# The opening of a fused spectral-filter and max-out kernel: an earlier sine, a row fix on another engine, split evacuations, and later x loads

## The chip, the cores and the metric

The kernel runs on one core of a Trainium2 chip. The time is device microseconds of one execution. An engine is named as in the profile: PE (matmul; PEld its weight loads), DVE (vector), ACT (scalar activation), POOL (GpSimd), SP (the queue that only issues DMAs).

## The reference: what is computed

```python
X = np.fft.rfft(x, axis=1)                  # x: 8 batches x 3072 x 256
y = np.fft.irfft(X * F, n=3072, axis=1)     # F = filt_r + 1j * filt_i, 1537 x 256
h = np.maximum(y @ w1, y @ w2)              # 24576 tokens, 256 -> 1024
out = h @ w_out                             # 1024 -> 256, float32
```

## The kernel before, in words

The transforms are done as matmuls with tables of sines. A length of 3072 is split as 96 times 32: a 96-point transform over one index (`f1`, in batch 0 `s1t`, from batch 2 on `s1` with folded inputs), an exchange of axes, then per frequency group a small transform with table `U` (`s2`), the product with the filter `F` (`products`), the inverse small transform with tables `VP` and `VQ` (`s3`, in batch 0 `s3t`), another exchange, and the inverse 96-point transform with table `G1` (`s4`, later `s4g`), which leaves y for a tile of 384 tokens, transposed. There are 8 tiles in a batch and 64 in all. The max-out layer uses max(a, b) = max(a - b, 0) + b: `moe_h` multiplies y by `Wd` = w1 - w2 and clips at 0, `moe_o` multiplies that by `Wo` and adds y times `M` = w2 w_out. `M` is made in the kernel from transposes of `w2b` (`prep_t`, lines 300 to 306) and a product (`prep_m`).

The order is written out by hand. An **opening** makes the tables and does the transforms of batch 0 without leaving the chip: `s1t` for 8 chunks of x, the transposes `t1` ("T1"), `table_v` and `put_v`, `s2`, the products, `s3t` for v = 1, 0, 2, 3, 4, 5, whose result is evacuated into the tile `zT`, and the transposes `t2` of zT into `zr`, which `s4` reads. Then a loop (lines 777 to 798) walks the 64 tiles in 8 steps each, a step having one `moe_h` (two matmuls), three or four matmuls of `moe_o` of the tile before, and whatever `todo` and `mid` hold for that step. These two lists are filled by `plan`, `plan_f1` and `plan_f2`: step numbers count from 0 to 63 within a batch. In batch 0 they hold, among others: `f1` of batch 1 (chunks 4 to 15 at steps 5 to 12) and its exchange read `f1_read` at step 13; `prep_t(0)` at step 7, `prep_t(1)` at step 8, `prep_m` at step 9; `load_xf` and `fold` of batch 2, which fetch x as float32 into one of three buffers XF and add and subtract halves on POOL; and `visit`, which does `s2`, the products and `s3` of the next batch from step 25 on.

What sets the order of the work around the change:

- Every engine works through its own instructions in program order and waits on semaphores. A DMA is issued from a queue of the engine that issues it: x chunks as bfloat16 (`load_x`), the filter and `Wo` from POOL, between POOL's computing; the raw filter rows, w1 and w2 (tile `WS`), the exchanges, and XF from SP.
- PSUM has eight banks: six in the pool `ps`, two in `pso`. A tile's first matmul waits until the bank's former content has been evacuated.
- In the filter table F, row 32 of the first frequency is special (the Nyquist row): `fix_f` (line 144) writes it over what `double_f` has copied there (line 128, four copies on DVE).
- The two halves of `U` are made by `sines_u(0)` and `sines_u(1)` on ACT (line 249). `table_v(0, ..)` and `s2` of v = 0 to 2 need the first, `table_v(1, ..)` and `s2` of v = 3 to 5 the second.
- `products` (line 657) gives each v two tiles: the first from PSUM on DVE; the second for v = 0, 2, 3, 4 on POOL from a copy `xs` that ACT makes (`stage_x`), for v = 1 on DVE, and for v = 5 shared between DVE (lines 396, 397) and POOL (line 398).
- `spin` and the extra matmuls of line 581 compute nothing that is used; they keep PE occupied.
- On POOL, after the products: `load_x(1, 2, 2)`, `load_wo`, `prep_wd(0)`, two more `load_x`, `prep_wd(1)` to `(3)`, then `cast_w2`, which makes the two halves of `w2b`, then `table_ct`. `prep_wd(q)` makes columns 256q to 256q + 255 of Wd, which `moe_h` needs from step 2q on.

Of the kernel before, what the change touches and what calls it, by code (L numbers as in the profile page):

```python
# [8 lines left out]
FP32 = mybir.dt.float32  # L9
BF16 = mybir.dt.bfloat16  # L10
AF = mybir.ActivationFunctionType
# [4 lines left out]
D = 256  # L16
HID = 1024
NP = 96
NM = 32
NW = 12  # L20
NU = 24
TWO_PI = 6.283184
# [5 lines left out]
def kernel(  # L28
# [23 lines left out]
    F = const.tile([128, 2, NW, 2, D], BF16)  # L52
# [24 lines left out]
    xb = {}  # L77

    def x_tile(b, c):
        if c % 2 == 0:  # L80
            xb[b] = xpool.tile([128, 8, D], BF16, tag="xb", name="xb")
        return xb[b][:, 4 * (c % 2):4 * (c % 2) + 4]

    def load_x(b, c, n):
        for k in range(c, c + n):
            xb[b, k] = x_tile(b, k)[0:NP]
        src = x[b].rearrange("(p m) d -> p m d", m=NM)
        m0 = 4 * (c % 2)
        G.dma_start(out=xb[b][0:NP, m0:m0 + 4 * n], in_=src[:, 4 * c:4 * c + 4 * n, :])  # L89
# [42 lines left out]
    FZ = XF[0][0:33, 0]  # L132
# [9 lines left out]
        G.tensor_copy(F[0:32, ri, 0, 0], FZ[0:32, ri])  # L142

    def fix_f():
        V.tensor_copy(F[32:33, 0, 0, 0], FZ[32:33, 0])


    V.memset(W1, 1.0)
    zero = init.tile([128, 1], FP32)
# [4 lines left out]
    jb = init.tile([128, 16], FP32)  # L154
    cid = init.tile([128, 128], FP32)

    hv = init.tile([128, 2, 1], FP32)
    load_x(0, 0, 1)
    G.iota(pid, pattern=[[1, 1]], base=0, channel_multiplier=1, allow_small_or_imprecise_dtypes=True)
# [32 lines left out]

    def table_ct():
        G.memset(CT, 0.0)
# [52 lines left out]
    def sines_u(h):  # L247
        uv = ua.rearrange("p u c s j -> p u (c s j)")
        S.activation(U[:, NW * h:NW * h + NW], uv[:, NW * h:NW * h + NW], AF.Sin, bias=zero, scale=TWO_PI)

    def table_g():
        pg = ps.tile([96, NP], FP32, tag="ps", name="pg")
        TE.matmul(pg, C1, I128[0:NP, 0:NP], start=True, stop=True)
        S.activation(G1, pg, AF.Copy)

    def table_v(h, q):
# [36 lines left out]
    def load_wo():  # L293
        G.dma_start(out=Wo, in_=moe_w_out.rearrange("(c p) j -> p c j", p=128))

    def prep_wd(q, engine):
        js = slice(256 * q, 256 * q + 256)
        engine.tensor_tensor(Wd[:, :, js], w1f[:, :, js], w2f[:, :, js], OP.subtract)
# [18 lines left out]
    bt = {}  # L317
# [2 lines left out]
    zd = {}  # L320
    at_ = {}

    def f1(b, c, engine):
        if c == 0:
# [3 lines left out]
        at = at_[b]  # L328
        pa = ps.tile([96, 2, D], FP32, tag="ps", name="pa")
        TE.matmul(pa, C1, xb[b, c // 2][:, 2 * (c % 2):2 * (c % 2) + 2], start=True, stop=True)  # L330
# [9 lines left out]
    def f1_read(b):  # L340
        bt[b] = bpool.tile([128, NU, D], BF16, tag="bt", name="bt")
        src = ad[b].rearrange("(u q) m d -> (q m) u d", q=4)
        for u0, u1 in ((0, 4), (4, 12), (12, NU)):
            nc.sync.dma_start(out=bt[b][:, u0:u1], in_=src[:, u0:u1])


    def s1(b, c):
# [140 lines left out]
    po = {}  # L488
# [86 lines left out]
            V.tensor_copy(bt[0][:, 4 * n:4 * n + 4], pb)  # L575

    def s3t(v, pq):
        pool, tag = (ps, "ps") if v % 2 else (pso, "po")
        pz = [pool.tile([128, 2, 2, 2, 2, NM], FP32, tag=tag, name="pt%d" % g) for g in range(2)]
        for _ in range(2 if v == 1 else 1):  # L580
            TE.matmul(pz[0].rearrange("p i s r c m -> p (i s r c m)"), W1[:, 0:128], W1, start=True, stop=True)  # L581
        for i in range(2):
            for s in range(2):
                for dc in range(2):
                    for q, tab in enumerate((VP, VQ)):
                        for g in range(2):
                            TE.matmul(pz[g][:, i, s, :, dc], pq[s][64 * g:64 * g + 64, q, i, 128 * dc:128 * dc + 128],  # L587
                                      tab[64 * g:64 * g + 64, 2 * v + i, s].rearrange("p (r m) -> p r m", r=2),
                                      start=(q == 0), stop=(q == 1))
        zv = zT.rearrange("p c m (w g) q -> p w g (c m) q", g=2)  # L590
        for g in range(2):
            o_ = zv[:, 2 * v:2 * v + 2, g]
            i_ = pz[g].rearrange("p i s r c m -> p i (c m) (s r)")
            if v >= 4 and g == 1:
                V.tensor_copy(o_, i_)
            else:
                S.activation(o_, i_, AF.Copy)

    def t2(c, engines):
        if c == 0:  # L600
            zr[0] = zrpool.tile([96, NM, D], BF16, tag="zr", name="zr")
        n = 4 // len(engines)
        for k, engine in enumerate(engines):
            pr = ps.tile([96, n, D], BF16, tag="ps", name="pr")
            m0 = 4 * c + n * k
            for m in range(n):
                for dc in range(2):
                    TE.transpose(pr[:, m, 128 * dc:128 * dc + 128], zT[:, dc, m0 + m].rearrange("p u q -> p (u q)"),  # L608
                                 I128)
            if engine is V:  # L610
                V.tensor_copy(zr[0][:, m0:m0 + n], pr)
            else:
                S.activation(zr[0][:, m0:m0 + n], pr, AF.Copy)

    def spin(n):
        for _ in range(n):
            pd = ps.tile([128, 512], FP32, tag="ps", name="pd")
            TE.matmul(pd, W1[:, 0:128], W1, start=True, stop=True)  # L618
# [84 lines left out]
    table_ct()  # L703
# [16 lines left out]

    todo = {}
# [1 line left out]
    def plan(b, step, fn, *a):  # L723
        todo.setdefault((b + step // 64, step % 64), []).append((fn, a))

    def plan_f1(b, nb, steps, read):
        for c, n in zip(range(4, 16), steps):
            plan(b, n, f1, nb, c, S if c % 2 == 0 else V)
        plan(b, read, f1_read, nb)

    mid = {}

# [15 lines left out]
            plan(b, steps[-1] + (6 if b else 11), s1_read, b + 2)  # L748

    plan(0, 1, t2, 1, (V,))  # L750
    plan(0, 7, prep_t, 0)
    plan(0, 9, prep_m)
    for c, n in ((2, 7), (4, 22), (5, 32), (6, 40), (7, 48)):
        plan(0, n, t2, c, (V,))
    plan_f1(0, 1, (5, 6, 7, 7, 9, 9, 10, 10, 11, 11, 12, 12), 13)
    plan_f2(0, (25, 28, 31, 35, 38, 42, 46), ((0,), (), (1,), (2,), (3,), (4,), (5, 6)),
            (8, 8, 10, 12, 17, 20, 24, 28), (10, 13, 16, 20, 24, 27, 30, 33))
    for b in range(1, B - 1):
        first = b == 1
        plan_f2(b, (15 if first else 14, 19 if first else 18, 23, 31, 34 if b < B - 2 else 35, 39, 47),  # L760
# [16 lines left out]
    for tt in range(8 * B + 1):  # L777
        b, i = divmod(tt, 8)
        k = 0
        for j in range(8):  # L780
# [48 lines left out]
```

## Time and profile before

| what | us |
|---|---|
| median of 3 runs (lowest, highest) | 497.7 (496.92, 498.1) |
| the profiled execution, its own time | 498.64 |
| its span, from the first instruction to the last | 496.8 |
| first `moe_h` matmul, from the span's start | 37.73 |
| first matmul of `prep_t(0)` | 41.64 |
| first matmul of `moe_o` | 44.19 |
| granted PE clock, mean over the span | 0.989 |

All times within the kernel are counted from the start of the span. The profile's views give, for each instruction or group of equal instructions, the engine, the line, the tiles written and read, the start and the duration; the idle time of the engine ahead of it, and what ended that idle time. `<-` stands between what is written and what is read. A table by stage gives the busy time of each engine and the granted share of PE's clock. A matmul's end is modelled, so that overlapping matmuls can fill a stage to 100%.

The DMAs of w1 and w2 are issued by SP at 25.07, 25.71, 26.25 and 26.76 us; each lands in sixteen parts, the last of them at 29.5, 33.42, 35.3 and 36.6 us. x chunk 2 of batch 1 is issued by POOL at 32.95 and lands at 39.76, Wo at 33.51 and 44.07, x chunks 4 and 6 at 35.65 and 45.71, 36.20 and 48.05.

### The profile page before, as it was taken

The numbers are of one execution on the slowest core, as the hardware profiler recorded it, in microseconds if no ns is written. First come the engines' busy times: TensorE is split into PE (matmuls) and PEld (weight loads), VectorE is DVE, ScalarE is ACT, GpSimd is POOL, SyncE is SP. The second block draws the span as 40 slices with busy tenths as digits, with TensorE's granted clock in tenths as the row PEclk, the third lists the DMA queues.
The fourth block names the chain that finished last, engine by engine and source line by source line (L and its number), as shares of the span: only waits on it lengthen the run. The fifth ranks groups of instructions, "written<-read, shape, count | busy, mean of one in ns | idle before, by whom it ended". The sixth has DMA issues, their size and how long they took to land.

```text
span 496.8 us, 14137 instructions
## 1 busy us (share of the span) xinstructions
PE 483.8 (97%) x5759; PEld 353.5 (71%) x5759; DVE 335.4 (68%) x535; ACT 320.4 (64%) x667; POOL 258.7 (52%) x342
## 2 busy tenths in 40 slices
PE   7699999999999999999999999999999999999997
PEld 3457777777777777777777777776777777777775
DVE  7886788468855688467855688457873688556542
ACT  5777478667775677576866668665766656464442
POOL 8694868318466594528646295536842212222220
PEclk9879999999999999999999999999999999999999
DMA  8989988996789867896789977897776834531112
GB/s 128 161 242 224 259 269 260 284 234 190 204 266 221 216 210 223 249 225 174 231 257 227 183 244 211 257 215 168 227 231 175 181 104 129 157 120 66 64 64 86
DMA packets 76626, 97.30 MB, mean 196 GB/s; under 512 B 7985, under 2 KB 54354, under 8 KB 75186
## 3 DMA queue, kind: packets, MB, share of 16 engines
q1 hardware_dynamic: 63218, 66.71, 52.1%
q0 software_dynamic: 13200, 29.60, 21.4%
q8 instruction: 45, 0.74, 0.7%
q14 instruction: 19, 0.16, 0.1%
q10 hardware_dynamic: 144, 0.09, 0.1%
HBM read 53.87 MB, written 47.19 MB: 203 GB/s over the span
## 4 chain that ended last, share of the span: by engine, by line
PE 92%; DMA 3%; ACT 2%; POOL 1%; issue 1%; DVE 0%; SPq 0%; POOLq 0%
PE po L536 34%; PE ph L482 33%; PE po L534 8%; PE pz L408 5%; PE pc L443 3%; PE px L384 2%; PE pa L355 2%; DMA xb<-in_x_dram 2%; DMA zr<-zd 1%; PE pt L587 1%; DMA zd<-zt 1%; PE pr L608 1%; POOL xb L89 1%; PE pt L581 1%; PE pa L330 1%
## 5 line engine op out<-in xcount | busy, mean ns | idle before, releaser
L486 ACT ACTIVATE gt<-ph 128x384 bf16<-128x384 f32 x357 | 175.7, 496 | 138.8 <-PE ph L482 136.2
L536 PE MATMUL po<-Wo,gt 128*128 128x256 bf16 x1528 | 262.7, 273 | 1.2 <-issue 1.2
L536 PEld LDWEIGHTS <-gt 128*128 128x128 bf16 x1528 | 144.7, 98 | 68.1 <-issue 13.5
L495 POOL DMA_DIRECT2D out_dram<-ot x186 | 103.1, 558 | 154.7 <-DVE ot L547 138.7
L390 DVE TENSOR_TENSOR pq<-px,F 128x1024 bf16<-128x1024 f32 x91 | 106.9, 1218 | 25.7 <-PE px L384 25.4
L484 DVE TENSOR_SCALAR gt<-ph 128x384 bf16<-128x384 f32 x155 | 83.6, 551 | 53.5 <-PE ph L482 47.1
L482 PEld LDWEIGHTS <-Wd 128*128 128x128 bf16 x1024 | 99.6, 98 | 13.7 <-issue 0.3
L104 POOL TENSOR_TENSOR xb<-XF 128x512 bf16<-128x512 f32 x48 | 61.3, 1277 | 66.9 <-DMA XF<-in_x_dram 31.7
L547 DVE TENSOR_SCALAR ot<-po 128x512 f32<-128x512 f32 x83 | 57.0, 686 | 35.0 <-PE po L536 33.1
L105 POOL TENSOR_TENSOR xb<-XF 128x512 bf16<-128x512 f32 x48 | 61.1, 1274 | 0.0
L359 ACT ACTIVATE at<-pa 128x512 bf16<-128x512 f32 x96 | 51.8, 611 | 3.4 <-PE pa L355 3.3
L412 ACT ACTIVATE zt<-pz 128x512 bf16<-128x512 f32 x84 | 45.6, 594 | 5.7 <-PE pz L408 1.9
L448 ACT ACTIVATE ce<-pc 128x384 f32<-128x384 f32 x56 | 23.7, 490 | 6.7 <-PE pc L443 6.0
L408 PE MATMUL pz<-pq,VP 64*64 64x256 bf16 x336 | 22.2, 281 | 0.0
L384 PE MATMUL px<-bt,U 64*64 64x256 bf16 x384 | 20.4, 283 | 1.2 <-ACT VQ L279 0.7
L408 PE MATMUL pz<-pq,VQ 64*64 64x256 bf16 x336 | 21.1, 269 | 0.0
L408 PEld LDWEIGHTS <-VP 64*64 64x64 bf16 x336 | 10.0, 105 | 13.3 <-issue 12.7
L355 PE MATMUL pa<-xb,CT 64*64 64x512 bf16 x192 | 18.0, 377 | 0.0
L443 PEld LDWEIGHTS <-zr 48*128 48x128 bf16 x896 | 13.1, 93 | 4.8 <-issue 4.4
L443 PE MATMUL pc<-G,zr 48*128 48x48 bf16 x896 | 15.4, 180 | 0.3 <-DMA zr<-zd 0.3
L384 PEld LDWEIGHTS <-U 64*64 64x64 bf16 x384 | 10.6, 109 | 3.9 <-issue 3.6
L618 PE MATMUL pd<-W 128*128 128x512 bf16 x28 | 9.2, 437 | 1.5 <-DVE zero L150 1.5
(383 smaller groups left out, 632.1 us busy)
## 6 DMA issues: line engine op xcount, KB each, us to landing
out_dram<-ot POOLq DMA_DIRECT2D x186, 128.0 KB, 3.8
XF<-in_x_dram SPq DMA_DIRECT2D x96, 192.0 KB
ad<-at SPq DMA_DIRECT2D x56, 192.0 KB
zd<-zt SPq DMA_DIRECT2D x42, 256.0 KB
zr<-zd SPq DMA_DIRECT2D x56, 192.0 KB
bt<-ad SPq DMA_DIRECT2D x13, 768.0 KB
WS<-in_moe_w_dram SPq DMA_DIRECT2D x4, 512.0 KB
xb<-in_x_dram POOLq DMA_DIRECT2D x8, 192.0 KB, 5.6
```

The source lines that it names most:

```text
L104: G.tensor_tensor(t_[:, 0], f[:, 0], f[:, 1], OP.add)
L105: G.tensor_tensor(t_[:, 1], f[:, 0], f[:, 1], OP.subtract)
L359: S.activation(at[:, m0:m0 + 2], pa[g], AF.Copy)
L390: E.tensor_tensor(pq, px.rearrange("p (o i) d -> p o i d", o=1).to_broadcast([128, 2, 2, D]), F[:, :, 2 * v:2 * v + 2, s], OP.mult)
L408: TE.matmul(pz[g][64 * s:64 * s + 64, i], tab[64 * g:64 * g + 64, 2 * v + i, s], pq[s][64 * g:64 * g + 64, q, i], start=(q == 0), stop=(q ...
L412: S.activation(zt[:, :, g], pz[g], AF.Copy)
L482: TE.matmul(ph, Wd[:, dc, 128 * j:128 * j + 128], y_[:, dc], start=(dc == 0), stop=(dc == 1))
L484: V.tensor_scalar(gt[tt][:, j], ph, 0.0, None, OP.max)
L486: S.activation(gt[tt][:, j], ph, AF.Relu)
L495: E.dma_start(out=dst, in_=ot[tt // 2][:, 3 * (tt % 2) + c])
L536: TE.matmul(p_, g_[:, n - 2, blk], Wo[:, n - 2], start=(e == 0), stop=(e == 9))
L547: V.tensor_scalar(ot[tt // 2][:, e - 1:e + 1], po[q // 2 % 2], SCALE, None, OP.mult)
```

## The change

In the opening:

- `fix_f` is done by POOL instead of DVE. In the built program it stands behind POOL's last filter DMA and ahead of its first product, and waits for the raw row and for the first of the four copies.
- A second sine on ACT writes the table of `C1` once more in another column order (tile `CP`), and `table_g` takes that one; so G1's rows, and the columns of zT, have a new order.
- `sines_u(1)` moves from behind `stage_x(2)` to ahead of `t1`. On ACT it stands behind the last evacuation of `s1t`.
- `s3t` takes its banks from `ps` for v = 0, 3, 5 and from `pso` for v = 1, 2, 4 (before: odd v from `ps`, even from `pso`). zT has a new layout, in eight blocks of four m; the matmuls write PSUM in that order (runs of 4 columns instead of 32), and for v = 5 each evacuation is split into the first block and the other seven.
- On POOL `prep_wd(0)` comes ahead of `load_x(1, 2, 2)`, `prep_wd(1)` ahead of `load_wo`, `prep_wd(2)` and `(3)` ahead of the last two `load_x`. `cast_w2` stays behind all of these.
- `f1` is cut into its matmul (`f1_in`) and its evacuation and DMA (`f1_out`). Three `f1_in` stand around `t2(0)` and one behind `s4(0)`, the evacuations behind `s4(0)` and at steps 1 and 2. The two `spin(1)` there become four matmuls into one bank of `pso`.

In batch 0: the exchange read of batch 1 goes out in its three pieces at steps 13, 14 and 15 instead of all at step 13, and the loads and folds of batch 2 get later steps.

```diff
     def fix_f():
-        V.tensor_copy(F[32:33, 0, 0, 0], FZ[32:33, 0])
+        G.tensor_copy(F[32:33, 0, 0, 0], FZ[32:33, 0])
...
         S.activation(C1, uc.rearrange("p k r -> p (k r)"), AF.Sin, bias=zero[0:NP], scale=TWO_PI)
+        S.activation(CP.rearrange("p (g w c) -> p g w c", g=2, c=4),
+                     uc.rearrange("p (w g s) r -> p g w (s r)", g=2, s=2), AF.Sin, bias=zero[0:NP], scale=TWO_PI)
...
     def s3t(v, pq):
-        pool, tag = (ps, "ps") if v % 2 else (pso, "po")
-        pz = [pool.tile([128, 2, 2, 2, 2, NM], FP32, tag=tag, name="pt%d" % g) for g in range(2)]
+        pool, tag = (ps, "ps") if v in (0, 3, 5) else (pso, "po")
+        pz = [pool.tile([128, 8, 2, 2, 2, 2, 4], FP32, tag=tag, name="pt%d" % g) for g in range(2)]
...
-        zv = zT.rearrange("p c m (w g) q -> p w g (c m) q", g=2)
-        for g in range(2):
-            o_ = zv[:, 2 * v:2 * v + 2, g]
-            i_ = pz[g].rearrange("p i s r c m -> p i (c m) (s r)")
+        for o0, o1 in ((0, 1), (1, 8)) if v == 5 else ((0, 8),):
+            for g in range(2):
+                o_ = zT[:, o0:o1, :, :, g, 2 * v:2 * v + 2].rearrange("p o c m w q -> p o (c m) (w q)")
+                i_ = pz[g][:, o0:o1].rearrange("p o i s r c m -> p o (c m) (i s r)")
...
-    zT = bpool.tile([128, 2, NM, NU, 4], BF16, tag="bt", name="zT")
+    zT = bpool.tile([128, 8, 2, 4, 2, NW, 4], BF16, tag="bt", name="zT")
+    sines_u(1)
     for n in range(6):
         t1(n, S if n % 2 else V)
...
     stage_x(2)
-    sines_u(1)
...
+    prep_wd(0, G)
     load_x(1, 2, 2)
+    prep_wd(1, G)
     load_wo()
-    prep_wd(0, G)
+    for q in range(2, 4):
+        prep_wd(q, G)
     for c in (4, 6):
         load_x(1, c, 2)
-    for q in range(1, 4):
-        prep_wd(q, G)
     for h in range(2):
         cast_w2(h)
...
-    f1(1, 0, S)
-    spin(1)
+    f1_in(1, 0)
+    fill(1)
     t2(0, (V, S))
-    f1(1, 1, V)
-    spin(1)
+    f1_in(1, 1)
+    f1_in(1, 2)
+    fill(1)
     s4(0)
-    f1(1, 2, S)
-    f1(1, 3, V)
+    f1_in(1, 3)
+    f1_out(1, 0, S)
+    f1_out(1, 1, V)
+    fill(2)
...
-        plan(b, read, f1_read, nb)
+        for k, (u0, u1) in enumerate(((0, 4), (4, 12), (12, NU))):
+            plan(b, read + k, f1_read, nb, u0, u1)
...
+    plan(0, 1, f1_out, 1, 2, S)
+    plan(0, 2, f1_out, 1, 3, V)
...
     plan_f2(0, (25, 28, 31, 35, 38, 42, 46), ((0,), (), (1,), (2,), (3,), (4,), (5, 6)),
-            (8, 8, 10, 12, 17, 20, 24, 28), (10, 13, 16, 20, 24, 27, 30, 33))
+            (8, 8, 13, 14, 19, 26, 32, 38), (10, 13, 23, 27, 32, 34, 37, 42))
```

`fill(n)` is n matmuls of 128x512 as in `spin`, all into one tile `pd` of `pso`.

More of the change, by code (lines that the diff above doesn't have):

```diff
@@ L155 @@
     cid = init.tile([128, 128], FP32)
+    CP = init.tile([NP, 96], BF16)
     hv = init.tile([128, 2, 1], FP32)
@@ L252, in table_g @@
         pg = ps.tile([96, NP], FP32, tag="ps", name="pg")
-        TE.matmul(pg, C1, I128[0:NP, 0:NP], start=True, stop=True)
+        TE.matmul(pg, CP, I128[0:NP, 0:NP], start=True, stop=True)
         S.activation(G1, pg, AF.Copy)
@@ L321, with f1_in, f1_out @@
     at_ = {}
+    pas = {}
     def f1(b, c, engine):
+        f1_in(b, c)
+        f1_out(b, c, engine)
+    def f1_in(b, c):
+        pas[c] = ps.tile([96, 2, D], FP32, tag="ps", name="pa")
+        TE.matmul(pas[c], C1, xb[b, c // 2][:, 2 * (c % 2):2 * (c % 2) + 2], start=True, stop=True)
+    def f1_out(b, c, engine):
         if c == 0:
@@ L327, in f1 @@
             at_[b] = apool.tile([128, 8, D], BF16, tag="at", name="at")
-        at = at_[b]
-        pa = ps.tile([96, 2, D], FP32, tag="ps", name="pa")
-        TE.matmul(pa, C1, xb[b, c // 2][:, 2 * (c % 2):2 * (c % 2) + 2], start=True, stop=True)
+        at, pa = at_[b], pas.pop(c)
         o_ = at[0:96, 2 * (c % 4):2 * (c % 4) + 2]
@@ L338, in f1, with f1_read @@
             nc.sync.dma_start(out=ad[b][:, 2 * c - 2:2 * c + 2], in_=at[0:96, m0:m0 + 4])
-    def f1_read(b):
-        bt[b] = bpool.tile([128, NU, D], BF16, tag="bt", name="bt")
+    def f1_read(b, u0, u1):
+        if u0 == 0:
+            bt[b] = bpool.tile([128, NU, D], BF16, tag="bt", name="bt")
         src = ad[b].rearrange("(u q) m d -> (q m) u d", q=4)
-        for u0, u1 in ((0, 4), (4, 12), (12, NU)):
-            nc.sync.dma_start(out=bt[b][:, u0:u1], in_=src[:, u0:u1])
+        nc.sync.dma_start(out=bt[b][:, u0:u1], in_=src[:, u0:u1])
     def s1(b, c):
@@ L577, in s3t @@
     def s3t(v, pq):
-        pool, tag = (ps, "ps") if v % 2 else (pso, "po")
-        pz = [pool.tile([128, 2, 2, 2, 2, NM], FP32, tag=tag, name="pt%d" % g) for g in range(2)]
+        pool, tag = (ps, "ps") if v in (0, 3, 5) else (pso, "po")
+        pz = [pool.tile([128, 8, 2, 2, 2, 2, 4], FP32, tag=tag, name="pt%d" % g) for g in range(2)]
         for _ in range(2 if v == 1 else 1):
-            TE.matmul(pz[0].rearrange("p i s r c m -> p (i s r c m)"), W1[:, 0:128], W1, start=True, stop=True)
+            TE.matmul(pz[0].rearrange("p o i s r c m -> p (o i s r c m)"), W1[:, 0:128], W1, start=True, stop=True)
         for i in range(2):
@@ L586, in s3t @@
                         for g in range(2):
-                            TE.matmul(pz[g][:, i, s, :, dc], pq[s][64 * g:64 * g + 64, q, i, 128 * dc:128 * dc + 128],
-                                      tab[64 * g:64 * g + 64, 2 * v + i, s].rearrange("p (r m) -> p r m", r=2),
+                            TE.matmul(pz[g][:, :, i, s, :, dc].rearrange("p o r m -> p r o m"),
+                                      pq[s][64 * g:64 * g + 64, q, i, 128 * dc:128 * dc + 128],
+                                      tab[64 * g:64 * g + 64, 2 * v + i, s].rearrange("p (r o m) -> p r o m", r=2, m=4),
                                       start=(q == 0), stop=(q == 1))
-        zv = zT.rearrange("p c m (w g) q -> p w g (c m) q", g=2)
-        for g in range(2):
-            o_ = zv[:, 2 * v:2 * v + 2, g]
-            i_ = pz[g].rearrange("p i s r c m -> p i (c m) (s r)")
[L594 to L597, printed above, removed]
+        for o0, o1 in ((0, 1), (1, 8)) if v == 5 else ((0, 8),):
+            for g in range(2):
+                o_ = zT[:, o0:o1, :, :, g, 2 * v:2 * v + 2].rearrange("p o c m w q -> p o (c m) (w q)")
+                i_ = pz[g][:, o0:o1].rearrange("p o i s r c m -> p o (c m) (i s r)")
+                if v >= 4 and g == 1:
+                    V.tensor_copy(o_, i_)
+                else:
+                    S.activation(o_, i_, AF.Copy)
     def t2(c, engines):
@@ L607, in t2 @@
                 for dc in range(2):
-                    TE.transpose(pr[:, m, 128 * dc:128 * dc + 128], zT[:, dc, m0 + m].rearrange("p u q -> p (u q)"),
+                    TE.transpose(pr[:, m, 128 * dc:128 * dc + 128],
+                                 zT[:, (m0 + m) // 4, dc, (m0 + m) % 4].rearrange("p g w q -> p (g w q)"),
                                  I128)
@@ L710, with fill @@
     gpool = ctx.enter_context(tc.tile_pool(name="gpool", bufs=2))
-    f1(1, 0, S)
-    spin(1)
+    pd = pso.tile([128, 512], FP32, tag="po", name="pd")
+    def fill(n):
+        for _ in range(n):
+            TE.matmul(pd, W1[:, 0:128], W1, start=True, stop=True)
+    f1_in(1, 0)
+    fill(1)
     t2(0, (V, S))
-    f1(1, 1, V)
-    spin(1)
+    f1_in(1, 1)
+    f1_in(1, 2)
+    fill(1)
     s4(0)
-    f1(1, 2, S)
-    f1(1, 3, V)
+    f1_in(1, 3)
+    f1_out(1, 0, S)
+    f1_out(1, 1, V)
+    fill(2)
     todo = {}
```

## The prediction, on record before the changed kernel ran

> **What bounds the kernel now.** I read the page first: PE is busy for 97% of the span, and the chain of work that ended last is PE for 92% of it.
>
> ```profile
> PE 483.8 (97%) x5759; PEld 353.5 (71%) x5759; DVE 335.4 (68%) x535; ACT 320.4 (64%) x667; POOL 258.7 (52%) x342
> ...
> PE 92%; DMA 3%; ACT 2%; POOL 1%; issue 1%; DVE 0%; SPq 0%; POOLq 0%
> ```
>
> Then the list of PE's waits. Each row is: who waited for whom, total us, times, longest.
>
> ```profile
> PE pv L265 <- ACT U L249: 1.5, 1, 1.5
> ...
> PE po L536 <- issue: 1.2, 1, 1.2
> ```
>
> Every wait of this list but two lies ahead of 38 us; those two are the 1.2 us above, which no semaphore ended (at 335 us), and one of 0.3 us for a DMA. The same list for 36 to 100 us is empty. So from the first matmul of `moe_h` (37.73 us) to the end at 496.8 us PE works through a fixed list. **Batch 0 has no wait that a better order could remove**; the change can gain only by letting that list start, and go on, sooner.
>
> The table by stage says why the opening is slow (columns: stretch, length, busy PE, PEld, DVE, ACT, POOL, then PEclk, DMA share, GB/s).
>
> ```profile
> 22.00:24.00 2.00, 0.46 (x11) 0.06 (x8) 1.78 (x4) 1.52 (x3) 0.80 (x2) 0.50 0.63 127
> ...
> 28.00:30.00 2.00, 2.00 (x45) 1.09 (x45) 2.00 (x3) 1.58 (x3) 2.00 (x2) 0.50 1.07 272
> ```
>
> PE idles at 22 to 24 us and then works at half clock until 31.4 us; DVE and POOL are full with the products. The last view is POOL's order of time (start, us, operation).
>
> ```profile
> 23.43 2.12 POOL L390 TENSOR_TENSOR pq<-xs,F 128x1024 bf16<-128x1024 f32 x1 [1.20 <-DVE F L128]
> 25.50 0.56 POOL L89 DMA_DIRECT2D xb<-in_x_dram  x1
> 26.07 6.30 POOL L390 TENSOR_TENSOR pq<-xs,F 128x1024 bf16<-128x1024 f32 x3
> 32.34 0.66 POOL L398 TENSOR_TENSOR pq<-xs,F 128x256 bf16<-128x256 f32 x1
> 32.95 0.56 POOL L89 DMA_DIRECT2D xb<-in_x_dram  x1
> 33.51 0.93 POOL L294 DMA_DIRECT2D Wo<-in_moe_w_out_dram  x1
> 34.43 1.30 POOL L298 TENSOR_TENSOR Wd<-WS 128x512 bf16<-128x512 f32 x1
> 35.65 1.06 POOL L89 DMA_DIRECT2D xb<-in_x_dram  x2
> 36.72 3.74 POOL L298 TENSOR_TENSOR Wd<-WS 128x512 bf16<-128x512 f32 x3
> 40.40 2.01 POOL L291 CAST w2b<-WS 128x1024 bf16<-128x1024 f32 x2
> ```
>
> From 23.43 to 42.41 us it has no gap. Its first `w2b` cast (1.03 us) ends at 41.43, and PE needs that half at once:
>
> ```profile
> 41.31 0.49 PE L482 MATMUL ph<-y__998,Wd 128*128 128x384 bf16 x2
> 41.64 0.61 PE L305 MATMUL pt<-I,w2b 128*128 128x128 bf16 x8
> ```
>
> The weight loads of `w2b` begin at 41.48, 0.05 us after the cast. **So two paths meet without slack at `prep_t(0)` (step 7): PE's own, and POOL's.** The change shortens the first. What it does to the second decides.
>
> **PE's path, part by part.**
> - *Sine ahead of T1.* ACT is idle from 15.08 to 16.43 us; the sine (0.93, L249) needs `ua`, done at 13.50, and fits: free there. If that cover went it would cost up to 0.93. In its old place (22.97 to 23.89) PE waited 1.5 us for it. Next late is the copy of `px` to `xs` (ends 23.07), so `table_v(1,0)`, `s2(0,3)` and `put_v(1,1)` come 1.2 to 1.5 us sooner; the last ends near 25.5 instead of 26.94.
> - *Second sine CP*: 0.38 (row L191), in ACT's idle time 4.32 to 6.08. Zero. `table_g` reads it 1 us later.
> - *Row fix on POOL.* On DVE it took 0.28 and the product behind it waited 0.19 more (23.25 to 23.76). DVE's products start about 0.45 sooner; both of v=1 are done at 25.65.
> - *Alternating banks.* Before, `s3t(2)` waited for banks that `s3t(0)` had filled one group earlier (released 31.17). Now its banks are those of `s3t(1)`, free at 28.2. With two fillers of 0.43 at half clock ahead, I get `s3t(1)` from 26.1 (was 26.94), `s3t(0)` 28.05 (29.02), `s3t(2)` 30.05 (31.25), `s3t(3)` 31.5 (32.25). `s3t(4)` needs POOL's fourth product (32.38): 32.45 (33.15). `s3t(5)`: filler 0.32 and 0.6 us behind it: 33.35 to 34.0 (was 34.69).
> - *Last tile in parts.* ACT takes 0.49 for 384 columns and 0.60 for 512, so the 64-column part costs 0.23 and the rest 0.54; DVE alike (0.55, 0.69). The first transposes wait for 0.23 and not for 0.6 to 0.7, and ACT comes to them with no queue: 34.4 instead of 35.59. Reading PSUM in another pattern is priced at zero: L564 reads 384 columns with a stride in the same 0.49 as L486 does in order.
> - *`f1` in halves, two more fillers (0.22 each).* They stand in PE's waits for zT, zr and y_. The four evacuations (0.58 and 0.68) go behind y_ on ACT and DVE, into the relus of tile 0; the transposes of `t2(1)` and the third ph wait for the banks of the first two, free 0.3 us earlier than needed.
>
> Sum: the first `moe_h` matmul at about 36.55 instead of 37.73, **1.2 us sooner** (0.7 from the products and banks, 0.5 from the parts). From there PE needs 3.9 us to `prep_t(0)`; waits of 0.3 to 0.4 for Wd's third and fourth quarters (38.7 and 39.95) come in, so it is there at 40.8.
>
> **POOL's path.** The operations between 23.43 and the cast are the same, so reordering cannot bring the cast ahead of 41.43. Two things push it back. (1) `prep_wd(0)` now stands first, at 33.0, and needs the first halves of w1 and w2: the trace has the last of their sixteen landings at 33.42. With the 0.1 us that POOL takes from such a wait to its start (23.33 to 23.43) that is 33.5; behind it the old steps: Wd 1.22, x 0.55, Wd 1.23, Wo 0.92, Wd 1.23 and 1.22, x 0.55 and 0.52, cast 1.03. **Cast done at 41.97 instead of 41.43.** In between these two DMAs wait longer: x chunk 2 is issued at 34.7 (was 32.95), Wo at 36.5 (33.51), the other x at 39.9 and 40.4 (35.65, 36.20). (2) The fix needs DVE's first copy only (19.71), stands behind POOL's last F issue (22.23), and takes 0.5 (row L142: 0.54). In the gap of 1.20 it is free; if DVE's fourth copy (to 23.25) keeps it out, everything on POOL is 0.45 later, the wait for the landing is gone, and the cast ends at about 41.95.
>
> For this the rows: POOL's four DMA issues at 18.82 to 22.23 took 1.0 to 1.28 each, all beside DVE's copies L128; the ones ahead of them took 0.49 to 0.58. [...]
>
> Both ways PE's first `w2b` transpose moves from 41.64 to about 42.1: **0.46 us later**, and the 1.2 us is spent waiting there (some 1.3 us). Behind it the list is the same. Ends: w1 and w2 landing ahead of 33.0 with the fix in the gap, 0; fix kept out and the landing 0.3 later, 0.75.
>
> **Wo and x.** Before, Wo landed at 44.07 and its first matmul started at 44.19. The queue was full from 34 to 48 us (DMA share 0.89 to 1.19): what lands when is set by the bytes ahead, not by the issue. Now x starts about 1.7 us later, but w1 and w2 get those engines, so I lose 0 to 0.7 us of transfer: Wo by 44.0 to 44.8, wanted at 44.65. Cost 0 to 0.15. x chunks 4 and 6 (45.71, 48.05) have 1.5 us to spare each.
>
> **Batch 0.** PE has no wait there, so the pieces of the exchange read gain nothing. They cost nothing while folds stay ahead of `s1`: the last fold goes from step 33 to 42, its load lands some 4.6 us after its issue at step 38 (62.17 to 66.75 us, a row of the same kind), the fold takes 2.55, and `s1` wants it at step 50, some 11 us after the issue.
>
> The profiled execution took 498.64 us (span 496.8); with 0.46 it would take 499.1. It lies 0.94 above the median of the runs shown, to which I add the same: 497.7 + 0.46 = **498.2 us**.
>
> **Rivals.**
> 1. *The cast does not hold PE* (spans on POOL are rough; the casts may end sooner than the rows say). Then the 1.2 us survives as far as Wo allows, 0.5 to 1.2: 496.5 to 497.2. Against it: the weight load stands 0.05 us behind the cast, so the row is good.
> 2. *Wo comes late* (the other side). If its 10.6 us from issue to landing are its own and not its queue's, it lands at 47.1 and PE waits 2.4 us at the first `moe_o`: 497.7 + 0.5 + 2.4 = 500.6. It decides once Wo lands after 44.65. For it: 44.07 against 44.19 is no slack at all. Against: of its 10.6 us the first 3.1 passed before w1 and w2 were out of the way.
> 3. *Strided PSUM writes.* `s3t` now writes runs of 4 columns where it wrote 32; no row here has such runs. If each group of 32 (0.57 us at full clock, 0.9 at half) took twice as long, six groups add some 4.4 us to PE's path, 3.1 beyond the wait it hides in: 501.3. [...]
> 4. *The fetch.* The 1.4 us that PE lost at 335 us had no semaphore behind it; five more PE instructions ahead of it could remove it or make another: 496.8 or 499.6.
>
> **How the numbers follow.** This kernel's measurement can tell about 0.2% (1.0 us) from no change. Forecast (0 to 0.75 later, 497.7 to 498.5): 0.55. Rival 1: 0.22, a third of it past the bound. Rival 2: 0.10. Rival 3: 0.05. Rival 4: 0.08, in halves. Faster: 0.07 of rival 1, 0.04 of rival 4 and 0.05 for a gain that I do not see, 0.16; slower: rivals 2 and 3, 0.04 of rival 4 and 0.02 of the forecast's far end, 0.21; same 0.63. The range leaves out rivals 2 and 3 and the edge of 1: 496.6 to 499.6.
>
> **What would show it.** Right: first `moe_h` matmul near 36.5; PE waiting 1 us or more for POOL at the `w2b` transposes; first cast done near 42.0; equal tile times after. Wrong: `w2b` cast before 41 us, PE waiting for Wo or xb by DMA, groups of `s3t` longer than 0.6 us at full clock, any PE wait in batch 0, or half clock outside 21 to 31 us.

## The result, and the profile after

The changed kernel takes 500.56 us (median of 8 runs, 499.19 to 501.63) against 497.88 us (496.92 to 498.76) for the kernel before beside it: a ratio of 1.0052, 95% interval 1.0037 to 1.0068. By the medians it is 2.7 us slower; 498.2 was forecast, and 500.56 lies above the range. The profiled execution took 501.3 us with a span of 499.5 us, 2.7 us more than that of before.

The page first: PE's busy time and the chain of work that ended last.

```profile
PE 485.0 (97%) x5757; PEld 354.8 (71%) x5761; DVE 335.1 (67%) x535; ACT 321.5 (64%) x669; POOL 260.1 (52%) x343
...
PE 87%; DMA 6%; POOL 4%; issue 1%; SPq 1%; ACT 0%; POOLq 0%; DVE 0%; ACTq 0%
```

PE's work is the same within 1.2 us, but its share of the chain fell from 92% to 87%, and DMA and POOL took what it lost. The chain view (start, us, what) lists its longest pieces; these three are among the new ones.

```profile
25.37 5.82 DMA F<-F
40.72 8.34 DMA xb<-in_x_dram
85.39 4.37 DMA XF<-in_x_dram
```

PE's waits between 34 and 110 us say where they reach PE. (In the kernel before this list is empty from 36 to 100 us.)

```profile
PE pt L308 <- POOL w2b L294: 0.7, 1, 0.7
PE pa L366 <- POOL xb L105: 0.6, 1, 0.6
PE pa L334 <- DMA xb<-in_x_dram: 0.5, 1, 0.5
PE pt L598 <- DVE pq L407: 0.3, 1, 0.3
```

The last row lies in the opening, ahead of the first `moe_h`. The rows count only time in which PE had nothing in flight. From start to start of its matmuls the other three losses are larger: the `w2b` transposes begin 0.8 us late, `f1` of chunk 8 is 0.6 late, `s1` at step 50 is 1.0 late. The starts of the tiles add them up: first `moe_h` matmul 38.10 us (37.73 before), tile 1 at 44.21 (42.97), tile 2 at 55.53 (53.56), tile 7 at 97.15 (94.14). The difference is 0.4, 1.2, 2.0 and 3.0 us, and nothing is added after that.

**The opening.** The stages shown before (columns as there):

```profile
22.00:24.00 2.00, 1.51 (x68) 0.82 (x55) 1.90 (x3) 1.93 (x4) 1.87 (x3) 0.55 0.64 114
28.00:30.00 2.00, 1.58 (x39) 1.14 (x39) 0.45 (x1) 0.93 (x3) 2.00 (x2) 0.50 0.99 243
```

The 1.5 us for the sine is gone (PE is busy for 1.51 of 22 to 24 us, was 0.46). But at 28 to 30 us DVE, full before, works for 0.45. POOL's order of time shows why.

```profile
22.77 0.39 POOL L145 CAST F<-XF 1x256 bf16<-1x256 f32 x1
...
25.32 0.56 POOL L89 DMA_DIRECT2D xb<-in_x_dram  x1
...
31.61 2.13 POOL L401 TENSOR_TENSOR pq<-xs,F 128x1024 bf16<-128x1024 f32 x1 [1.50 <-DMA F<-F]
...
34.32 1.27 POOL L301 TENSOR_TENSOR Wd<-WS 128x512 bf16<-128x512 f32 x1
...
40.72 1.05 POOL L89 DMA_DIRECT2D xb<-in_x_dram  x2
41.77 2.03 POOL L294 CAST w2b<-WS 128x1024 bf16<-128x1024 f32 x2
```

POOL and DVE stood still until 31.6 us (from 30.1 and 28.5) for the filter rows of v = 4, which SP copies within SBUF (`F<-F`, four DMAs). The fourth landed at 31.2 us, 5.8 us after its issue; before, at 26.8, 2.3 us after its issue. So the first cast ends at 42.82 (41.43 before), and PE, which is done with the `moe_h` ahead of it, gets its transposes at 42.87:

```profile
42.87 0.62 PE L308 MATMUL pt<-I,w2b 128*128 128x128 bf16 x8 [0.66 <-POOL w2b L294]
```

**Batch 0.** SP's DMAs and POOL's folds around step 50:

```profile
79.10 1.85 SPq L94 DMA_DIRECT2D XF<-in_x_dram  x2
81.06 0.93 SPq L424 DMA_DIRECT2D zd<-zt  x2
82.52 0.81 SPq L373 DMA_DIRECT2D ad<-at  x2
83.37 2.68 SPq L94 DMA_DIRECT2D XF<-in_x_dram  x2
```

```profile
89.89 1.27 POOL L104 TENSOR_TENSOR xb<-XF 128x512 bf16<-128x512 f32 x1 [3.53 <-DMA XF<-in_x_dram]
91.12 1.26 POOL L105 TENSOR_TENSOR xb<-XF 128x512 bf16<-128x512 f32 x1
```

```profile
91.39 0.40 PE L366 MATMUL pa<-xb,CT 64*64 64x512 bf16 x1
92.43 0.41 PE L366 MATMUL pa<-xb,CT 64*64 64x512 bf16 x3 [0.64 <-POOL xb L105]
```

The load of batch 2's last chunk stands in the plan at step 38, whose first matmul starts at 77.60 us, but SP issues it at 83.37 to 86.05. Ahead of it in SP's queue stand the load of the next batch's first chunk (79.10), which waits for its buffer until the fold of chunk 5 ends at 79.07, and four exchange writes. The load's own buffer was free at 75.5, when the fold of chunk 4 ended. From then to 79.1 SP stood for the other load's buffer, and until 83.4 it issued that load and the four writes, with 0.5 us of waiting for the data of the last two. The load lands near 89.8; the fold holds PE by 1.0 us. In the kernel before, where this load came ahead of the next batch's, the same fold was done some 10 us before PE read it:

```profile
77.05 1.27 POOL L104 TENSOR_TENSOR xb<-XF 128x512 bf16<-128x512 f32 x1
78.28 1.26 POOL L105 TENSOR_TENSOR xb<-XF 128x512 bf16<-128x512 f32 x1
```

```profile
89.42 0.41 PE L355 MATMUL pa<-xb,CT 64*64 64x512 bf16 x4
```

So the theory to test: three waits add up, one per moved group (POOL's order, the x loads behind it, batch 0's plan), and the opening's own edits bring little. Rivals: one delay of the opening that only shows at three places; the late `F<-F` copy alone; PE's own work (strided writes).

### The profile page after: what moved, and what is told of

Same layout as the page of the kernel before. It is cut to its first block, busy times and chain, and to the rows that moved or that the text cites. A ratio compares the mean times of both kernels' runs of the same rounds, so it can differ in the third digit from the quotient of the medians.

```text
span 499.5 us, 14141 instructions
## 1 busy us (share of the span) xinstructions
PE 485.0 (97%) x5757; PEld 354.8 (71%) x5761; DVE 335.1 (67%) x535; ACT 321.5 (64%) x669; POOL 260.1 (52%) x343
## 4 chain that ended last, share of the span: by engine, by line
PE 87%; DMA 6%; POOL 4%; issue 1%; SPq 1%; ACT 0%; POOLq 0%; DVE 0%; ACTq 0%
PE po L547 34%; PE ph L493 32%; PE po L545 8%; PE pz L419 5%; PE pc L454 3%; PE pa L366 2%; PE px L395 2%; DMA xb<-in_x_dram 2%; DMA F<-F 1%; DMA F<-in_filt_r_dram 1%; POOL F L122 1%; POOL xb L89 1%; POOL Wd L301 1%; DMA XF<-in_x_dram 1%; DMA F<-in_filt_i_dram 1%
## 5 line engine op out<-in xcount | busy, mean ns | idle before, releaser
L556 DVE COPY ot<-po 128x512 f32<-128x512 f32 x12 | 8.2, 685 | 3.9 <-PE po L547 3.0
```

## The experiments

Each kernel was timed beside the kernel before (medians 497.78 to 497.92 us); "ratio" is to that, with its 95% interval. The start of the first T1 transpose, which hangs on x landing, lies between 14.37 and 16.49 us in the profiles; so I compare the time from it to the first `moe_h` matmul ("T1 to moe_h"), the length of tiles 0 and 1 together, and step 50 (start to start of `moe_h`), as PE's rows give them. These three columns are from one profiled execution each. Runs of one kernel lie 2 to 6 us apart, so two edited kernels whose intervals overlap are not told apart.

| kernel | ratio (interval) | median us | T1 to moe_h | tiles 0 + 1 | step 50 |
|---|---|---|---|---|---|
| before | 1 | 497.88 | 22.59 | 15.83 | 1.21 |
| changed | 1.0052 (1.0037 to 1.0068) | 500.56 | 23.59 | 17.43 | 2.24 |
| plan_old | 1.0029 (1.0014 to 1.0044) | 499.74 | 22.89 | 16.69 | 1.21 |
| load7_early | 1.0041 (1.0022 to 1.0059) | 499.90 | 22.52 | 16.76 | 1.21 |
| pool_old | 1.0037 (1.0017 to 1.0058) | 499.68 | 22.15 | 16.28 | 2.95 |
| both_old | 1.0004 (0.9989 to 1.0020) | 498.24 | 22.61 | 15.88 | 1.21 |
| b_plan | 1.0019 (1.0000 to 1.0038) | 499.17 | 23.41 | 16.01 | 2.16 |
| b_pool | 1.0030 (1.0015 to 1.0044) | 499.09 | 23.07 | 16.46 | 1.21 |
| fix_dve | 1.0008 (0.9989 to 1.0026) | 497.87 | 21.99 | 16.25 | 1.21 |
| warm | 0.9990 (0.9975 to 1.0005) | 498.23 | 23.34 | 15.99 | 1.21 |
| x_later | 1.0005 (0.9990 to 1.0020) | 497.68 | 24.72 | 15.82 | 1.21 |
| bal | 0.9988 (0.9972 to 1.0004) | 497.32 | 21.60 | 16.07 | 1.21 |
| bal_x | 1.0018 (0.9996 to 1.0040) | 498.44 | 22.11 | 15.82 | 1.21 |
| bal_all | 1.0023 (1.0005 to 1.0041) | 498.91 | 23.73 | 16.95 | 1.21 |

### Taking the parts back: plan_old, pool_old, both_old

plan_old gives the changed kernel batch 0's old plan:

```diff
-            (8, 8, 13, 14, 19, 26, 32, 38), (10, 13, 23, 27, 32, 34, 37, 42))
+            (8, 8, 10, 12, 17, 20, 24, 28), (10, 13, 16, 20, 24, 27, 30, 33))
...
-        for k, (u0, u1) in enumerate(((0, 4), (4, 12), (12, NU))):
-            plan(b, read + k, f1_read, nb, u0, u1)
+        for u0, u1 in ((0, 4), (4, 12), (12, NU)):
+            plan(b, read, f1_read, nb, u0, u1)
```

> The changed kernel with batch 0's steps of before: loads and folds of batch 2 at the old steps, the exchange read in one step. Theory (three waits add up: w2b cast and start 1.2 us, x chunk 4 0.7, the last fold of batch 2 1.0): the PE wait of s1 for POOL at 91.4 us goes, tiles 5 to 7 start with the same spacing as before, and the time is 1.0 less than the changed kernel's 500.6, so 499.5. Rival (the fold row is only where a delay shows that the opening makes; another wait takes its place): 500.3 to 500.6.

Measured 0.8 us less than the changed kernel, where 1.0 was expected (the two intervals overlap a little); step 50 is back at 1.21.

pool_old gives it POOL's old order behind the products:

```diff
-    prep_wd(0, G)
     load_x(1, 2, 2)
-    prep_wd(1, G)
     load_wo()
-    for q in range(2, 4):
-        prep_wd(q, G)
+    prep_wd(0, G)
     for c in (4, 6):
         load_x(1, c, 2)
+    for q in range(1, 4):
+        prep_wd(q, G)
```

> The changed kernel with POOL's old order behind the products (x chunk 2, Wo, Wd 0, x chunks 4 and 6, Wd 1 to 3, casts). Theory: x chunk 4 lands by 46 to 47 us and the f1 of chunk 8 does not wait (0.6 to 0.7 us less); the cast comes no earlier, since POOL does the same operations ahead of it: still done near 42.8 and waited for 0.7. So 499.9. Rival 1 (the early Wd is what holds the cast, by waiting for w1 and w2): cast done at 42 or before, 499.2. Rival 2 (Wd 0 to 3 now late for moe_h, which starts sooner than before): waits of moe_h for Wd take the gain away, 500.6.

Measured 0.9 less by the medians, but the intervals overlap, so the size is not settled. x chunk 4 lands at 44.73 us (49.06 in the changed kernel), and nothing waits for it. The cast ends at 40.80, not near 42.8: rival 1 is right that the cast comes sooner, but mostly because in this execution POOL's fourth product did not wait. Part of what PE gained, it gave back at step 50: 2.95 instead of 2.24. PE reached that step 2.7 us sooner (88.23), and the load of the last chunk landed only 2.0 us sooner (87.72). **A wait for a landing grows when PE comes sooner by more than the landing does.** So two waits of this kind don't add fully when one is taken away.

both_old has both edits.

> The changed kernel with both old: POOL's order and batch 0's steps; only the opening's edits on PE, ACT, DVE (sine, banks, parts, f1 halves, row fix on POOL) are left. Theory (waits add): 500.6 - 0.7 - 1.0 = 498.9, still 1.0 over before, because the cast is as late as in the changed kernel (filter rows of v = 4 land late). If that late landing is only that one execution's: 497.9, equal to before. Rival (the opening's own edits cost PE time, by strided writes or fillers): 499.5 or more with the tile spacing of before.

Measured 1.0004: not told apart from the kernel before. The 498.9 of the theory did not come, and the 497.9 for a late landing of one execution alone was near: the cast is done at 41.71 here. The two plans carry the loss; the opening's edits on PE, ACT and DVE neither cost nor gain anything that can be measured. The rival (strided writes) is out. A group of 32 matmuls of `s3t` in fix_dve (below), at full clock, starts at 30.59 and its last pair at 31.04; before, 32.25 and 32.70: the same 0.45 us, with runs of 4 columns as with 32.

### Adding the parts to the kernel before: b_plan, b_pool

b_plan is the kernel before with the new plan and the read in three steps; b_pool is the kernel before with the new POOL order (the two diffs above, the other way round).

> The kernel before with only batch 0's steps of the change: exchange read in three steps, loads and folds of batch 2 later. Theory (the late load of the last chunk costs by itself): PE waits 1 us or more for the last fold of batch 2 near 91 us, and the time is 1.0 to 1.4 over the kernel before: 499.0. Rival (the wait shows only with the changed opening): no wait at s1, 497.8.

> The kernel before with only POOL's order of the change (Wd 0 ahead of x chunk 2, Wd 1 ahead of Wo, the x of chunks 4 and 6 behind Wd 3). Theory: x chunk 4 lands some 2 us later than before and f1 of chunk 8 waits for it, the cast comes 0 to 0.5 later: 0.7 to 1.5 over the kernel before, so 498.9. Rival (it was only the late filter rows of v = 4 that pushed POOL and the x loads back): within 0.3 of before, 497.9.

The times came as both theories had them, +0.19% and +0.30% (b_plan's interval just reaches no change). With both_old's 0.04% the parts sum to 0.53%, and the whole measured 0.52%; each of these is uncertain by 0.15 to 0.2%. b_plan waits at the same place as the changed kernel (PE's order of time):

```profile
91.03 0.41 PE L355 MATMUL pa<-xb,CT 64*64 64x512 bf16 x3 [0.56 <-POOL xb L105]
```

In b_pool the wait for x chunk 4 that was expected did not come: it landed at 47.31 us, and its first `f1` starts at 49.03. The first loss is one that the changed kernel's profile hides, since there POOL was itself late: POOL, with its products done at 33.79 us, stands until w1 and w2 have landed, and PE then stands for the cast.

```profile
34.99 1.27 POOL L298 TENSOR_TENSOR Wd<-WS 128x512 bf16<-128x512 f32 x1 [1.20 <-DMA WS<-in_moe_w_dram]
```

```profile
43.53 0.62 PE L305 MATMUL pt<-I,w2b 128*128 128x128 bf16 x8 [0.46 <-POOL w2b L291]
```

Its longer T1 to moe_h (23.07) is not the order's doing: ahead of that, at 34.62 us, PE stood for 0.7 us in the middle of `s3t(4)` with no semaphore to end it.

Behind this new order PE meets the cast, Wo and x chunk 4, all close to their time, and which one it waits for differs from profile to profile: cast 0.7 and x 0.5 in the changed kernel, cast 0.6 in plan_old, cast 0.3 and Wo 0.3 in load7_early. Tiles 0 and 1 take 16.46 to 17.43 us with it, in all four; 15.83 to 16.28 in the other five of the first nine rows.

### One load moved: load7_early

```diff
-            (8, 8, 13, 14, 19, 26, 32, 38), (10, 13, 23, 27, 32, 34, 37, 42))
+            (8, 8, 13, 14, 19, 26, 32, 33), (10, 13, 23, 27, 32, 34, 37, 42))
```

> The changed kernel with one step moved: the load of batch 2's last chunk at step 33 instead of 38, its fold still at step 42. Theory (the load is late because on SP it stands behind the exchange writes, which wait for their data): the load is issued ahead of 80 us, the fold is done ahead of 87 us, PE's wait of 1.0 us at s1 goes: 499.5. Rival (the fold is late on POOL, by its step 42, or the landing is late however early it is issued): the fold still ends past 90 us and the time stays at 500.3 to 500.6.

The wait at `s1` is gone, so the load was the late one, and not POOL (the fold itself ended at 89.79, not ahead of 87 as I expected, and that was early enough). The edit takes the load past both the next batch's load and the exchange writes; that the former held it most is read from SP's rows above. But six loads now stand together on SP, and the exchange writes come behind them, from 82.55 us (81.06 in the changed kernel):

```profile
73.14 8.91 SPq L94 DMA_DIRECT2D XF<-in_x_dram  x6
```

and the readers of that exchange wait in this profile (PE's waits from 38 to 130 us):

```profile
PE pc L454 <- DMA zr<-zd: 1.0, 1, 1.0
PE px L395 <- DMA bt<-ad: 0.9, 1, 0.9
```

The time, 1.0041, can't be told from the changed kernel's. That these waits come from this order is likely, but not shown: one profile has them.

### Why the opening gained nothing: fix_dve, warm

fix_dve is both_old with the row fix on DVE again.

```diff
-        G.tensor_copy(F[32:33, 0, 0, 0], FZ[32:33, 0])
+        V.tensor_copy(F[32:33, 0, 0, 0], FZ[32:33, 0])
```

> The changed kernel with POOL's order and batch 0's steps of before, and also the row fix back on DVE. Theory (the fix on POOL starts DVE's products 0.4 sooner, but POOL is kept from its own first product by 0.1, and POOL's fourth product holds s3t of v = 4): no difference beyond the noise, 498.2. Rival 1 (the fix on POOL, drawn out beside DVE's copies, is what eats the opening's gain): 497.6. Rival 2 (it is worth the 0.4 that DVE gains): 498.6.

1.0008: no difference in time. In the profile T1 to moe_h is 21.99, the shortest of the first nine. The rows show two causes; how much each brings was not measured, since this profile also has a shorter stretch at half clock (below), and pool_old reached 22.15 with the fix on POOL. First the fix on POOL in both_old:

```profile
22.42 1.23 POOL L145 CAST F<-XF 1x256 bf16<-1x256 f32 x1
```

It started beside DVE's last copy (22.17 to 23.40) and took 1.23 us; in the changed kernel, behind the copies, 0.39. It took 1.23 to 1.33 in five of the seven profiles that have it on POOL, and in each of the five it ends 0.25 us after the copy beside which it started. What draws it out there no run shows. DVE's first product starts 0.10 us after its last copy (0.51 before), POOL's first 0.34 (0.18 before). And POOL's chain of four products is what `s3t` of v = 4 waits for once PE is fast (warm, below).

Second, the order in which banks come free. In both_old (and in every other profile with the fix on POOL and no fillers) `s3t(0)` starts, and its second matmul waits: its second bank is the one that `s2` of v = 4 filled and ACT copies to `xs`, behind two evacuations (27.11 to 28.20).

```profile
28.12 0.23 PE L598 MATMUL pt<-VP,pq 64*128 64x64 bf16 x1
28.74 0.21 PE L598 MATMUL pt<-VP,pq 64*128 64x64 bf16 x1 [0.38 <-ACT xs L666]
```

```profile
28.08 0.61 ACT L666 ACTIVATE xs<-px 128x512 f32<-128x512 f32 x1
```

With the fix on DVE the wait isn't there: `s3t(0)` goes through from 27.48 us while ACT makes that copy (27.43 to 28.03), so its banks are others. Counted by PE's starts, `s3t(1)` to `s3t(2)` takes 4.35 us (25.21 to 29.56), against 4.74 (26.05 to 30.79); before it was 4.31. So, with the fix on POOL, "alternating banks" took away one wait (`s3t(2)` for `s3t(0)`) and put another in.

warm is both_old with seven fillers in PE's idle time:

```diff
+    pw = pso.tile([128, 512], FP32, tag="po", name="pw")
+    pxs = {v: s2(0, v, (pw, 2) if v == 0 else ()) for v in (1, 0)}
+    TE.matmul(pw, W1[:, 0:128], W1, start=True, stop=True)
...
+    pxs[2] = s2(0, 2, (pw, 4))
```

(`s2` puts that many fillers behind its first matmul.)

> The changed kernel with POOL's order and batch 0's steps of before, and seven more fillers of 128x512 on PE in its idle time between 18.9 and 22 us. Theory (PE's stretch at half clock, 10.2 us long in every profile, begins after PE has idled there and then covers s3t; at full clock s3t of v = 0, 2, 3 takes 0.57 and not 0.8 a group): the half clock is gone or begins 3.4 us later, first moe_h matmul 22.0 us or less after the first T1 transpose (22.5 to 22.6 without), time 497.6. Rival (fillers change neither the clock nor the end, since the casts and POOL's products hold PE): 498.2; fillers in the way of real work: 498.5.

The clock did what was expected. Stages of half a microsecond of the kernel before (the clock is the third number from the end) give the edges of its slow stretch:

```profile
21.00:21.50 0.50, 0.09 (x1) 0.04 (x1) 0.50 (x1) 0.50 (x2) 0.50 (x1) 0.79 0.66 97
31.50:32.00 0.50, 0.50 (x31) 0.45 (x25) 0.50 (x2) 0.16 (x1) 0.50 (x1) 0.97 1.12 320
```

A mean of 0.79 over half a microsecond means 0.29 at full clock (the stages on either side show 1.00 and 0.50): from 21.29 to 31.53, 10.24 us. Worked out the same way the stretch of fix_dve runs from 23.07 to 29.90 us, 6.83. The stretch begins anywhere between 21.3 and 23.8 us in the first nine profiles, whatever the kernel: before, b_plan and b_pool have the same opening, and theirs begin at 21.29, 21.47 and 23.82. In warm, PE's clock is full from 15 us, where the stages begin, to 33.3. Half clock follows and still holds at 36.0, where they end; by the granted clock of 0.997 over the span of 496.8 us I estimate it at 3.5 us at most. A stage that lay at half clock before is at full clock here:

```profile
26.00:28.00 2.00, 1.15 (x34) 0.60 (x36) 2.00 (x3) 1.57 (x3) 1.99 (x2) 1.00 0.54 55
```

PE is faster and so waits: for POOL's and DVE's products and for ACT's copy of `px` (1.1, 0.9 and 0.9 us in the list of this profile, in which the rows of v = 4 were late again). T1 to moe_h is 23.34, not the 22.0 expected, and 0.9990 is not told apart from before. So in this profile PE's speed is not the bound of the opening; POOL's chain and the landing of the last filter rows are. With the rows in time this was not tried for the fillers alone.

### The late filter rows: x_later

In the first ten profiles the fourth `F<-F` copy lands 2.2 to 2.3 us after its issue in six, and 4.5 to 5.8 us after it in four. The four are those where POOL's load of x chunks 0 and 1 was issued before the copy or beside it (changed: x at 25.32, copy at 25.37; plan_old 25.26 and 25.39; b_plan 25.14 and 25.32; warm 25.67 and 25.64); in the six the copy is 0.7 to 1.2 us ahead. b_plan has the opening of the kernel before: **so this is not the change's doing**; it falls to either kernel, by which of the two is issued first (the copy waits for the last filter load and goes at 24.1 to 25.6 us). That the x load is what delays the copy is a guess from this order. x_later moves that x load behind POOL's product of v = 2 (and the `f1` matmuls that need it behind `t2`), in both_old.

```diff
-        if v == 0:
+        if v == 2:
             load_x(1, 0, 2)
```

> The changed kernel with POOL's order and batch 0's steps of before, and x chunks 0 and 1 of batch 1 issued by POOL behind its product of v = 2 instead of v = 0 (the four f1 matmuls that read them stand behind t2 instead of one ahead of it). Theory (in the profiles where the fourth copy of filter rows is issued at the time of that x load or after it, the rows of v = 4 land near 31 us and POOL idles 1 us or more; where the copy is 0.7 us or more ahead, they land near 27): POOL goes from its third product to its fourth without a gap, and the slow end of the runs goes: 497.8, highest under 499.3. Rival (the x lands too late for f1, or the copies are late for another reason): 498.5 or a gap on POOL as before.

POOL goes through without a gap: the x load between, and the last two products from 31.28 to 35.50 us.

```profile
26.55 4.21 POOL L401 TENSOR_TENSOR pq<-xs,F 128x1024 bf16<-128x1024 f32 x2 [2.39 <-ACT VP L282]
30.71 0.56 POOL L89 DMA_DIRECT2D xb<-in_x_dram  x1
```

But that execution had x and the filter rows late from the start (T1 at 16.49, DVE's copies from 21.46), and the time is 1.0005 with a highest run of 500.94 (under 499.3 was expected): the slow end did not go.

### Towards a faster kernel: bal, bal_x, bal_all

bal: warm with the row fix on DVE, and the second product of v = 5 on DVE altogether, so that POOL has 0.66 us less ahead of Wd.

```diff
         if v == 5:
-            pq.append(shared_product(v, 1, pxs[v][1], xs[v], pool))
+            pq.append(product(V, v, 1, pxs[v][1], pool))
```

> The kernel with seven more fillers, and besides the row fix on DVE and all of the v = 5 product on DVE, so that POOL's chain ahead of Wd and the casts is 0.66 + 0.15 to 0.35 shorter. Theory (POOL's chain is what held the opening's gain): the first w2b cast ends 17.0 us after DVE's last copy of filter rows instead of 18.3, the first moe_h matmul comes 21.6 us after the first T1 transpose, time 497.2. Rival (DVE now holds s3t of v = 5, or x and Wo by DMA hold PE): 498.0.

The profile comes near the theory: T1 to moe_h 21.60, first cast done 17.5 us after DVE's last copy (40.83 and 23.30; 18.2 before, 17.0 expected), and the list of PE's waits from 36 to 130 us is empty. The time, 0.9988 (0.9972 to 1.0004), is the lowest of all, but its interval still reaches no change.

bal_x adds x_later's move; bal_all adds to that `prep_t` one step later, `prep_m` at step 10, and Wd 1 to 3 mixed with the x loads.

> The kernel of the last expectation with the x load of the one before it (x chunks 0 and 1 behind the product of v = 2). Theory (both costs are real and add): 496.8, with the highest run under 498.5. Rival (x by DMA becomes the wait at f1): 497.5 to 498.

> The kernel of the last expectation, and prep_t one step later, prep_m at step 10 instead of 9, and on POOL Wd 1, 2 and 3 mixed with the x loads of chunks 4 and 6. Theory (Wd and the casts on POOL are what PE waits for in the first tile): tile 0 takes 5.2 us or less from its first moe_h matmul, no PE wait for w2b or Wd, 496.4. Rival (M comes late for the first moe_o, or x chunk 4 lands late): a wait of 0.3 to 1 at moe_o or f1, 497.2.

Both missed. bal_x took 1.0018 with five of its twelve runs above 499 us; its one profile (496.9 us) shows only a wait of 0.5 us for x at `f1`, so what makes the others slow stays open. bal_all took 1.0023: its profile has Wd 0 and Wd 2 waiting for w1 and w2, which landed as late as 39.84 us (36.6 in the kernel before), and the fourth copy landing 4.4 us after its issue with no x load ahead of it. So an x load ahead is not the only cause of a late copy.

## Why the prediction was wrong, point by point

- *Batch 0, "they cost nothing while folds stay ahead of `s1`", "some 11 us after the issue".* **This step failed.** I took the step of the plan (38, at 77.6 us) for the issue. SP works in order, and the load stood behind a load that waited 3.6 us for a buffer and behind four exchange writes: issued 83.37 to 86.05, landed 89.8, 1.0 us of wait. The 4.6 us to the landing were misread too: 66.75 is the first of that load's sixteen parts, and the last came at 68.39, 6.2 us after the issue; here it took 6.4 from the first issue. The 11 us were, if anything, too few: from step 38 to step 50 the kernel before takes 13.4 us (75.62 to 89.00). b_plan alone costs 0.19%, about 0.9 us, where the sum had nothing. The working weighed POOL's queue, which the reordering passes, and not SP's.
- *POOL's path, "0.46 us later".* The mechanism was right and the size off: the new order alone cost 0.30% (b_pool), 1.5 us; in the four profiles with it tiles 0 and 1 are 0.6 to 1.6 us longer, by the cast, Wo or x. **This term was too small.** "Cast done at 41.97", counted from T1, is 26.83 us; load7_early has 26.84 (42.31 at T1 15.47), so the number is right where the rows come in time. In b_pool it is 27.55, since w1 and w2 landed 1.2 us after POOL wanted them (I had allowed 0.5, 0.3 more at the far end), in the changed kernel 28.31 by the late rows of v = 4. The other way that was given, 0.45 by a fix that the copies keep out, is there as well: POOL's first product starts 0.64 us after DVE's last copy (0.18 before), and the wait for the rows hides it.
- *"x chunks 4 and 6 have 1.5 us to spare."* **Failed** in the changed kernel: issued 5.07 us later, chunk 4 landed 3.35 later (49.06), and PE waited. I had argued that bytes ahead and not the issue set the landing. In plan_old, load7_early and b_pool it landed at 46.98, 47.70 and 47.31 with no wait, 0.9, 0.6 and 1.7 us ahead of its reader (1.4 before): the new order alone did not make it late. In the changed kernel it is issued 0.7 to 1.5 us later than in these, counted from T1, and takes 8.3 us to land against 5.9 to 7.5.
- *Wo.* Landed at 45.49, first `moe_o` at 45.53: no cost here, 0.3 in load7_early. The rival that gave 500.6 by a late Wo met the time by chance; its mechanism did not happen.
- *Opening, "1.2 us sooner".* The parts were right: the sine's wait is gone, DVE's products start 0.41 sooner against its copies, `s3t(5)` to `t2(0)` fell from 1.09 to 0.63 us (0.5 forecast). The sum was not: T1 to moe_h is 22.15 to 22.61 in the three profiles with the new opening and the rows of v = 4 in time, 22.59 and 23.07 in the two with the old one (the latter with the gap of 0.7). What took it, as far as the rows show: 0.4 us at `s3t(0)` by the new banks, POOL's chain 0.15 later, and a clock stretch whose place I had taken from one profile. What each is worth in time was not measured.
- *Rivals.* Strided writes: no cost, 0.45 us a group in both; the doubling that its 501.3 was worked out from was assumed, and no run shows it. The fetch: 1.2 us at one place in batch 5 in the changed kernel as before (the working's 1.4 is 1.2 in the list of waits), so it changed nothing here. The cast does hold PE.

## What to carry to other kernels

A step in a plan is not the time of an issue: find what stands ahead on that queue, and what those instructions wait for, before giving a load "11 us"; and read its landing from the last of its parts, not the first. A list in which PE never waits says that each landing is in time, not by how much; every load that is moved needs its own slack, from the row of its landing against the row of its first reader. And a gain at the head of a chain is worth only what the landings behind it allow: pool_old came 2.7 us sooner to step 50 and waited 0.7 longer there.

## What the runs showed of the hardware

- The half-clock stretch of PE is 10.2 us long in seven of the first nine profiles and 6.8 in two (b_pool and fix_dve); it starts at 21.3 to 23.8 us. In the four profiles with seven fillers of 0.22 us in the idle time ahead of it, it does not begin there: two (warm and bal_all) go to half clock at 33.3 and 33.5 us and are still there at 36.0, where the stages end; two (bal and bal_x) have none, with a granted clock of 1.000 over the span.
- The fourth copy within SBUF issued by SP lands 2.2 to 2.3 us after its issue in eight profiles, 2.9 in one, and 4.4 to 5.8 in five, in four of these with a large load from POOL's queue just ahead or beside it.
- POOL's CAST of one row of 256 takes 0.39 us alone and 1.23 to 1.33 when it starts beside one of DVE's copies of 32x4096.
